# One maximum and one exponential for the longest query tile of an attention, with a new order of its steps

## The chip, the cores and the metric

The kernel runs on one core of a Trainium2 chip. The metric is the time of one execution on the device in microseconds (us). Engines are named as in the profile: PE is TensorE (matrix products, and transposes as products with a unit matrix), DVE is VectorE, ACT is ScalarE, POOL is GpSimd, and SP is SyncE, whose queue issues nearly all of the transfers.

## The reference

Three layers follow one another: a block-causal attention, a dense FFN with an ELU, and a mixture of experts that gives each token to one expert. The change touches the attention alone.

```python
B, H, S, D = 2, 8, 576, 64
scores = np.matmul(q, k.transpose(0, 1, 3, 2)) / np.sqrt(D)
mask = (np.arange(S)[:, None] // 64) >= (np.arange(S)[None, :] // 64)
scores = np.where(mask, scores, -1e9)
scores = scores - np.max(scores, axis=-1, keepdims=True)
attn = np.exp(scores)
attn = attn / (np.sum(attn, axis=-1, keepdims=True) + 1e-09)
x = np.matmul(attn, v)                    # then (1152, 512), all heads side by side
h = x @ w_in                              # (512, 2048)
x = np.where(h > 0, h, np.exp(np.minimum(h, 0)) - 1) @ w_out
...                                       # then the mixture of 8 experts
```

## The kernel before

A matrix product of two float32 operands is made of products of a high and a low part of each (q, k and the values are split so). The 16 heads are worked on in 8 pairs: head a of a pair sits in partitions 0 to 63 of q and k, head b in 64 to 127.

The queries of a head are cut in five tiles of 128 (the first has 64). Tile t has as many keys as the mask leaves it: 64, 192, 320, 448 and 576. The scores lie in PSUM in three parts: part 0 is tile 4, whose 576 keys take two banks of 288 each; part 1 is tile 3 (448 keys) with tile 0 (64 keys) in one bank; part 2 is tiles 2 and 1 (320 and 192 keys) in one bank. With two banks for transposes and two for the values, all eight banks are taken.

The attention's instructions come in an order that is written out by hand: a string of 115 steps, `ORDER`, is worked through once per round, and each engine has its share of the steps in just this order. The last digit of a step says how many pairs it lies behind: round i does step `...1` for pair i-1, so a pair is spread over up to four rounds. There are 11 rounds (0 to 10), of which the middle ones hold all steps. The letter before the last digit is the head. The steps, with the lines of the profile:

- `S` scores (PE, L423; the mask is added by a product of its own, L434); `Spi` is piece i of part p, so `S00` and `S01` are the two banks of tile 4.
- `M` the maximum of a piece over its keys, negated (DVE, `largest`, L445); `M02` is the smaller of the two negated maxima of tile 4 (`largest_of_two`, L452).
- `E` the exponential, with the sum of a row along with it (ACT, `power`, L458).
- `D` the denominators on DVE: `D02` adds the two sums of tile 4 (L465), then `total` adds 1e-9 (L473) and `inverse` inverts (L479).
- `N` the normalization of the probabilities (POOL, L485).
- `T`, `TE` transposes of probabilities on PE (L504, L508, L529), `t`, `te` their evacuation (ACT L495 for t00, t10 and te0, DVE L496 for the others).
- `V` the value products (PE, L545), `X` their evacuation (ACT L560, DVE L87).
- `K` transposes of q and k of the next pair (PE, L370), `k` their split into high and low (ACT L378, DVE L379), `B` the copy of k for both heads (POOL, L339), `L` and `Q` transfers on SP's queue that stack the parts of k and q (L358, L350).
- `c` conversion steps of the FFN's first weights, on ACT, DVE and POOL.

Transfers are issued by the same steps: behind the second `V` of a pair v of a later pair is loaded (L316, L319), behind the second `Q` raw q and k. SP's queue issues one after the other in this order. A step whose input isn't there holds back what stands behind it on its engine. The FFN and the experts come after this, from other code.

Of the kernel before, what the change touches and what calls it, by code (L numbers as in the profile page):

```python
# [9 lines left out]
FP32 = mybir.dt.float32  # L10
# [4 lines left out]
ACTF = mybir.ActivationFunctionType  # L15
# [11 lines left out]
D00a1 S00b1 E20b1 S01b1 M11b1 K0a0 M01b1 N21a1 D01a1 K1a0 M00b1 k00a0 k01a0 X003 k10a0 N11a1 N10a1  # L27
V12 D02a1 E11b1 D20b1 M02b1 E10b1 N00a1 E01b1 k11a0 L0 K0b0 X013 c52 c32 D21b1 k00b0 c73 T1a1 S20a0
S21a0 E00b1 S10a0 S11a0 t11a1 D10b1 k01b0 D11b1 TEa1 M21a0 t10a1 D00b1 M20a0 c62 N20b1 D01b1 c00
M11a0 D02b1 T2a1 te0a1 S00a0 S01a0 t21a1 E20a0 t20a1 T0a1 E21a0 K1b0 M10a0 M00a0 X102 t00a1 k10b0  # L30
M01a0 D20a0 N00b1 N11b1 X112 E10a0 N21b1 V02 k11b0 T0b1 c11 M02a0 N10b1 t00b1 D21a0 S20b0 S21b0 B00
B30 E11a0 T2b1 c41 Q00 c21 E00a0 T1b1 E01a0 B20 t21b1 t20b1 S10b0 S11b0 B10 Q10 t11b1 t10b1 M20b0
M21b0 D10a0 M10b0 TEb1 te0b1 N20a0 E21b0 D11a0
# [9 lines left out]
def attention_ffn_moe(  # L43
# [231 lines left out]
    def part1():  # L275
# [84 lines left out]
        def turn(m, which, g, pool=ps_t, tag="t"):  # L360
# [6 lines left out]
            bank = pool.tile([128, 512], FP32, tag=tag, name="qkT")  # L367
# [39 lines left out]
        def scores(n, part, i):  # L407
# [3 lines left out]
            if c0 == 0:  # L411
                banks[n, part, b] = ps_s.tile([128, 512], FP32, tag=f"s{part}{b}", name="s")
            bank, (q0, nq) = banks[n, part, b], QT[t]
# [27 lines left out]

        def largest(n, part, i):
            t, b, c0, k0, w = PIECES[part][i]
            nq = QT[t][1]
            nc.vector.tensor_reduce(  # L445
                out=stat[n][0][0:nq, t + b:t + b + 1], in_=banks[n, part, b][0:nq, c0:c0 + w], axis=AX.X,
                op=ALU.max, negate=True,
            )

        def largest_of_two(n, t):  # L450
            neg = stat[n][0]
            nc.vector.tensor_tensor(out=neg[:, t:t + 1], in0=neg[:, t:t + 1], in1=neg[:, t + 1:t + 2], op=ALU.min)  # L452

        def power(n, part, i):
            prob[n, part] = PROB[part][n % 2]
            t, b, c0, k0, w = PIECES[part][i]
            nq = QT[t][1]
            nc.scalar.activation(  # L458
                out=prob[n, part][0:nq, c0 + k0:c0 + k0 + w], in_=banks[n, part, b][0:nq, c0:c0 + w], func=ACTF.Exp,
                bias=stat[n][0][0:nq, t:t + 1], accum_out=stat[n][1][0:nq, t + b:t + b + 1],  # L460
            )

        def total_of_two(n, t):
            den = stat[n][1]
            nc.vector.tensor_tensor(out=den[:, t:t + 1], in0=den[:, t:t + 1], in1=den[:, t + 1:t + 2], op=ALU.add)  # L465
# [11 lines left out]
        def inverse(n, part):  # L477
            rd = stat[n][2][:, cols(part)]
            nc.vector.reciprocal(out=rd, in_=rd)  # L479
# [112 lines left out]
        for _ in range(42):  # L592
            nc.tensor.matmul(out=warm[:, 0:128], lhsT=mrow, rhs=mrow, start=True, stop=True)
        for w in "kq":
            for g in range(2):
                for f in turn(0, w, g, ps_s, ("s10", "s20", "s00", "s01")[2 * "kq".index(w) + g]):
                    f()
# [32 lines left out]
        def do(name, h, m):  # L630
# [31 lines left out]
            elif kind == "M":  # L662
                largest_of_two(n, 4) if rest == [0, 2] else largest(n, *rest)
            elif kind == "E":
                power(n, *rest)
            elif kind == "D":
                if rest == [0, 0]:
                    total_of_two(n, 4)
                elif rest[1] == (1 if rest[0] == 0 else 0):
                    total(n, rest[0])  # L670
                else:
                    inverse(n, rest[0])
# [686 lines left out]
```

## Time and profile before

| | before |
| --- | --- |
| median of 3 executions | 496.95 us (495.81 to 499.03) |
| the profiled execution | 498.9 us, of it 496.6 between the first and the last instruction |
| PE busy | 475.1 us (96%) |
| PE's weight loads | 396.1 us (80%) |
| DVE busy | 346.7 us (70%) |
| ACT busy | 308.5 us (62%) |
| POOL busy | 117.2 us (24%) |
| mean granted clock of TensorE, as a share of full speed | 0.994 |

The attention takes the first 110 us or so. Its rounds begin, by the split of a pair's k on ACT, at 8.97, 18.49, 29.76, 41.45, 53.12, 64.79 and 76.45 us. Busy times overlap: an engine takes up an instruction before the last is done, so lengths of neighbours add up to more than the time from start to start. A busy PE waits for nothing, but its ends are modelled. In rows of a timeline the bracket tells how long the engine was idle just before and what it was inferred to wait for.

### The profile page before, as it was taken

Reading aid. Unit: us, or ns where it says so; the run is one execution under the profiler, and the core shown is the slowest. Engines: PE = TensorE matmul, PEld = TensorE weight load, DVE = VectorE, ACT = ScalarE, POOL = GpSimd, SP = SyncE. Lnnn points to the kernel's source line nnn. Section 1 sums busy time; section 2 is a strip of 40 time slices with the busy share of each in tenths; the row PEclk is TensorE's granted clock in tenths of the full one; section 3 lists DMA queues with packets and bytes.
Section 4 is the critical chain, followed back from the end, with each engine's and each line's share of the span. In section 5 each row is a group of like instructions: output and inputs, shape, how many; then the busy total and the mean of one; then the engine's idle time right before and its main releaser. Section 6 shows DMA issues by size and latency. Waiting matters only on the chain. (4 is left out here: it accounts for less than half of the span.)

```text
span 496.6 us, 8643 instructions
## 1 busy us (share of the span) xinstructions
PE 475.1 (96%) x2822; PEld 396.1 (80%) x2822; DVE 346.7 (70%) x841; ACT 308.5 (62%) x696; POOL 117.2 (24%) x209
## 2 busy tenths in 40 slices
PE   6899999999999999999999999999999999999993
PEld 6778887879998898999999888877777777775772
DVE  6789897969978999994373465458378985551560
ACT  4788997867856667654463446437388884642650
POOL 6467877560000000000000020421111331210210
PEclk9999999999999999999999999989999999999999
DMA  8789775503789975341023032529969999350100
GB/s 192 165 206 216 168 173 109 149 21 114 176 241 260 295 264 170 98 128 42 1 85 86 0 107 52 187 79 361 390 208 319 354 364 316 100 215 21 29 26 24
DMA packets 61253, 80.85 MB, mean 163 GB/s; under 512 B 33170, under 2 KB 33170, under 8 KB 61200
## 3 DMA queue, kind: packets, MB, share of 16 engines
q1 hardware_dynamic: 58368, 75.18, 50.7%
q0 software_dynamic: 1632, 4.72, 2.5%
q8 instruction: 28, 0.46, 0.4%
q10 hardware_dynamic: 1200, 0.30, 0.3%
q14 instruction: 25, 0.20, 0.1%
HBM read 62.17 MB, written 12.41 MB: 150 GB/s over the span
## 5 line engine op out<-in xcount | busy, mean ns | idle before, releaser
L260 PE MATMUL acc<-wbh,gh 128*128 128x512 f32 x144 | 57.3, 398 | 0.0
L260 PE MATMUL acc<-wbh,gl 128*128 128x512 f32 x144 | 57.1, 397 | 0.0
L260 PE MATMUL acc<-wbl,gh 128*128 128x512 f32 x144 | 57.1, 397 | 0.0
L916 POOL DMA_INDIRECT disp<-y_all,slot x9 | 9.2, 1019 | 200.6 <-DVE e L245 177.9
L485 POOL TENSOR_SCALAR prob<-prob,stat 128x576 f32<-128x576 f32 (+3 forms) x80 | 42.3, 542 | 27.8 <-DVE stat L479 18.6
L458 ACT ACTIVATE prob<-s,stat 128x288 f32<-128x288 f32 (+4 forms) x96 | 45.3, 480 | 1.5 <-POOL kk L339 0.8
L243 ACT ACTIVATE e<-h 128x384 f32<-128x384 f32 x48 | 23.3, 485 | 36.5 <-PE h L233 34.1
L87 DVE TENSOR_TENSOR xl<-ra,xh 128x1024 fp32r<-128x1024 f32 (+1 forms) x36 | 39.3, 1100 | 8.8 <-ACT xh L1128 6.9
L186 DVE SCALAR_TENSOR_TENSOR cv_t<-r,cv_t 128x512 int32<-128x512 int32 x64 | 44.1, 690 | 0.3
L1262 POOL DMA_INDIRECT out<-o,gt x12 | 17.0, 1413 | 112.2 <-DVE o L1261 68.8
L233 PE MATMUL h<-xh,wah 128*128 128x384 f32 x192 | 42.2, 341 | 0.8 <-DVE e L245 0.8
L233 PE MATMUL h<-xl,wah 128*128 128x384 f32 x192 | 41.6, 337 | 0.0
L245 DVE SCALAR_TENSOR_TENSOR e<-e,h 128x384 f32<-128x384 f32 x48 | 26.4, 549 | 21.3 <-ACT e L244 21.1
L233 PE MATMUL h<-xh,wal 128*128 128x384 f32 x192 | 41.1, 336 | 0.0
L445 DVE TENSOR_REDUCE stat<-s 128x1 f32<-128x288 f32 (+4 forms) x96 | 37.6, 422 | 2.8 <-PE s L434 1.6
L1229 PE MATMUL acc<-xh,gh 128*128 128x512 f32 (+1 forms) x96 | 39.4, 411 | 0.0
L1128 ACT ACTIVATE xh<-ra 128x1024 fp32r<-128x1024 f32 (+1 forms) x36 | 34.4, 963 | 7.3 <-PE h L233 2.8
L87 DVE TENSOR_TENSOR xl<-rb,xh 128x1024 fp32r<-128x1024 f32 (+1 forms) x36 | 38.8, 1099 | 0.1
L233 PEld LDWEIGHTS h<-xh,wah 128*128 128x128 f32 x192 | 34.2, 188 | 5.7 <-DVE e L245 1.7
L1229 PE MATMUL acc<-xh,gl 128*128 128x512 f32 (+1 forms) x96 | 37.9, 395 | 0.0
L1229 PE MATMUL acc<-xl,gh 128*128 128x512 f32 (+1 forms) x96 | 37.9, 395 | 0.0
L87 DVE TENSOR_TENSOR gl<-hT,gh 128x512 fp32r<-128x512 f32 (+1 forms) x24 | 15.8, 657 | 29.9 <-ACT gh L1223 29.8
(173 smaller groups left out, 1165.9 us busy)
## 6 DMA issues: line engine op xcount, KB each, us to landing
ra<-in_moe_w SPq DMA_DIRECT2D x32, 512.0 KB, 5.3
rb<-in_moe_w SPq DMA_DIRECT2D x32, 512.0 KB, 6.6
r<-in_moe_w_in SPq DMA_DIRECT2D x16, 512.0 KB, 5.1
r<-in_moe_w_out SPq DMA_DIRECT2D x16, 512.0 KB, 4.4
disp<-z SPq DMA_DIRECT2D x18, 257.0 KB, 7.2
rows<-disp SPq DMA_DIRECT2D x14, 257.0 KB, 3.6
out<-z SPq DMA_DIRECT2D x9, 256.0 KB, 4.9
kr<-in_k SPq DMA_DIRECT2D x16, 128.0 KB, 2.8
```

Of the source, the lines that this page charges most:

```text
L87: eng.tensor_tensor(out=lo, in0=x, in1=hi.bitcast(FP32), op=ALU.subtract)
L186: nc.vector.scalar_tensor_tensor(out=st["t"], in0=x(), scalar=scalar, in1=st["t"], op0=op, op1=ALU.bitwise_or)
L233: nc.tensor.matmul(out=h[:, f, :], lhsT=w[:, kk, (f0 + f) * 128:(f0 + f + 1) * 128], rhs=x[:, kk, t0:t0 + n], start=(i == 0), stop=(i == l ...
L243: nc.scalar.activation(out=e, in_=hf, func=ACTF.Relu, scale=-1.0)
L245: nc.vector.scalar_tensor_tensor(out=e, in0=e, scalar=-1.0, in1=hf, op0=ALU.add, op1=ALU.max)
L260: nc.tensor.matmul(out=acc[t], lhsT=x[:, f, t * 128:(t + 1) * 128], rhs=w[:, f0 + f, :], start=(first and f == 0 and i == 0), stop=(last a ...
L445: nc.vector.tensor_reduce(out=stat[n][0][0:nq, t + b:t + b + 1], in_=banks[n, part, b][0:nq, c0:c0 + w], axis=AX.X, op=ALU.max, negate=True,)
L458: nc.scalar.activation(out=prob[n, part][0:nq, c0 + k0:c0 + k0 + w], in_=banks[n, part, b][0:nq, c0:c0 + w], func=ACTF.Exp, bias=stat[n][0 ...
L485: nc.gpsimd.tensor_scalar(out=p, in0=p, scalar1=stat[n][2][0:nq, t:t + 1], scalar2=0.0, op0=ALU.mult, op1=ALU.add)
L1128: lambda: nc.scalar.activation(out=hi, in_=r, func=ACTF.Copy),
L1229: nc.tensor.matmul(out=acc[0:n], lhsT=x[:, f % 4, 0:n], rhs=y[:, f % 2, :], start=(f == 0 and i == 0), stop=(f == NF - 1 and i == 2),)
L1262: nc.gpsimd.indirect_dma_start(out=views[e * CT + j], out_offset=bass.IndirectOffsetOnAxis(ap=gate[e][0:n, j, 1:2].bitcast(I32), axis=0), ...
```

## The change

Tile 4's two banks become one PSUM tile `[128, 2, 512]`. One reduction over both axes gives the maximum of 576 scores, and one activation all 576 exponentials and their sum; `largest_of_two` and `total_of_two` go, and with them the steps M01, M02, E01 and D02. The prologue takes its four banks from a list that is put up first; they are the same banks in the same order. The 107 steps that are left stand in a new order. In it all steps keep the digit that says in which round they are done, that is, a step moves within its round alone.

```diff
--- before.py
+++ after.py
@@ -24,13 +24,12 @@
 
 
 ORDER = """
-D00a1 S00b1 E20b1 S01b1 M11b1 K0a0 M01b1 N21a1 D01a1 K1a0 M00b1 k00a0 k01a0 X003 k10a0 N11a1 N10a1
...
+D00a1 N21a1 S00b1 K0a0 k00a0 S01b1 k01a0 c73 N11a1 N10a1 D01a1 K1a0 c52 V12 E20b1 k10a0 E10b1 B00
...
 """
 
 ON_ACT = {"t00", "t10", "te0"}
@@ -357,14 +356,15 @@
                 own = slice(64 * h, 64 * h + 64)
                 nc.sync.dma_start(out=KLO[m % 2][own, h].bitcast(FP32), in_=kT[m][1][own].bitcast(FP32))
 
-        def turn(m, which, g, pool=ps_t, tag="t"):
+        def turn(m, which, g, bank=None):
 
             src, dst, sc = (qraw, qT, SCALE) if which == "q" else (kraw, kT, 1.0)
             if g == 0:
                 dst[m] = tuple(qt_p.tile([128, S], F32R, tag=which + x, name=which + x) for x in "hl")
             js = range(NK)[2 * g:2 + (NK - 2) * g]
             a, e = 128 * js[0], min(S, 128 * (js[-1] + 1))
-            bank = pool.tile([128, 512], FP32, tag=tag, name="qkT")
+            if bank is None:
+                bank = ps_t.tile([128, 512], FP32, tag="t", name="qkT")
             ps = bank[:, 0:e - a]
             for j in reversed(js):
                 nc.tensor.transpose(
@@ -408,9 +408,9 @@
 
             m, h = divmod(n, 2)
             t, b, c0, k0, w = PIECES[part][i]
-            if c0 == 0:
-                banks[n, part, b] = ps_s.tile([128, 512], FP32, tag=f"s{part}{b}", name="s")
-            bank, (q0, nq) = banks[n, part, b], QT[t]
+            if c0 == 0 and b == 0:
+                banks[n, part] = ps_s.tile([128, 2 if part == 0 else 1, 512], FP32, tag=f"s{part}", name="s")
+            bank, (q0, nq) = banks[n, part][:, b], QT[t]
 
             wq = 128
             if m:
@@ -439,30 +439,25 @@
 
             return mask
 
+        def whole(n, part, i):
+
+            t, c0 = parts[part][i]
+            nb, w = split(t)
+            return banks[n, part][0:QT[t][1], 0:nb, c0:c0 + w], slice(t, t + 1), slice(0, QT[t][1])
+
         def largest(n, part, i):
-            t, b, c0, k0, w = PIECES[part][i]
-            nq = QT[t][1]
-            nc.vector.tensor_reduce(
-                out=stat[n][0][0:nq, t + b:t + b + 1], in_=banks[n, part, b][0:nq, c0:c0 + w], axis=AX.X,
-                op=ALU.max, negate=True,
-            )
-
-        def largest_of_two(n, t):
-            neg = stat[n][0]
-            nc.vector.tensor_tensor(out=neg[:, t:t + 1], in0=neg[:, t:t + 1], in1=neg[:, t + 1:t + 2], op=ALU.min)
+            s, t, r = whole(n, part, i)
+            nc.vector.tensor_reduce(out=stat[n][0][r, t], in_=s, axis=AX.XY, op=ALU.max, negate=True)
 
         def power(n, part, i):
             prob[n, part] = PROB[part][n % 2]
-            t, b, c0, k0, w = PIECES[part][i]
-            nq = QT[t][1]
+            s, t, r = whole(n, part, i)
+            c0 = parts[part][i][1]
+            nk = s.shape[1] * s.shape[2]
             nc.scalar.activation(
-                out=prob[n, part][0:nq, c0 + k0:c0 + k0 + w], in_=banks[n, part, b][0:nq, c0:c0 + w], func=ACTF.Exp,
-                bias=stat[n][0][0:nq, t:t + 1], accum_out=stat[n][1][0:nq, t + b:t + b + 1],
+                out=prob[n, part][r, c0:c0 + nk].rearrange("q (b w) -> q b w", b=s.shape[1]), in_=s, func=ACTF.Exp,
+                bias=stat[n][0][r, t], accum_out=stat[n][1][r, t],
             )
-
-        def total_of_two(n, t):
-            den = stat[n][1]
-            nc.vector.tensor_tensor(out=den[:, t:t + 1], in0=den[:, t:t + 1], in1=den[:, t + 1:t + 2], op=ALU.add)
 
         def cols(part):
             ts = [t for t, _ in parts[part]]
@@ -591,9 +586,11 @@
         warm = ps_v.tile([128, half], FP32, tag="v0", name="warm")
         for _ in range(42):
             nc.tensor.matmul(out=warm[:, 0:128], lhsT=mrow, rhs=mrow, start=True, stop=True)
+        free = [ps_s.tile([128, x, 512], FP32, tag=f"s{i}", name="qkT") for i, x in ((1, 1), (2, 1), (0, 2))]
+        free = [x[:, i] for x in free for i in range(x.shape[1])]
         for w in "kq":
             for g in range(2):
-                for f in turn(0, w, g, ps_s, ("s10", "s20", "s00", "s01")[2 * "kq".index(w) + g]):
+                for f in turn(0, w, g, free.pop(0)):
                     f()
         load_qk(2)
         for _ in range(4):
@@ -660,16 +657,11 @@
                 if name != "S20":
                     pend[n, name]()
             elif kind == "M":
-                largest_of_two(n, 4) if rest == [0, 2] else largest(n, *rest)
+                largest(n, *rest)
             elif kind == "E":
                 power(n, *rest)
             elif kind == "D":
-                if rest == [0, 0]:
-                    total_of_two(n, 4)
-                elif rest[1] == (1 if rest[0] == 0 else 0):
-                    total(n, rest[0])
-                else:
-                    inverse(n, rest[0])
+                (inverse if rest[1] else total)(n, rest[0])
             elif kind == "N":
                 norm(n, *rest)
             elif kind == "T":
```

What the string of steps moves is seen on the engines. First SP's queue in round 5 (`kl` and `qq` are the stacked low k and the stacked q of the next pair, the first two `qq` being head a's, `v_114` the values of a later pair, `r` raw FFN weights). Before:

```order
L151 DMA r<-in_moe_w_in 128x2x512
L358 DMA kl_125<-kl 64x576 x2
L316 DMA v_114<-in_v 128x4x64 x2
L319 DMA v_114<-in_v 64x2x64
L350 DMA qq<-qh 64x576
L350 DMA qq<-ql 64x576
L350 DMA qq<-qh 64x576
L350 DMA qq<-ql 64x576
```

and in the changed kernel:

```order
L150 DMA r<-in_moe_w_in 128x2x512
L357 DMA kl_125<-kl 64x576 x2
L349 DMA qq<-qh 64x576
L349 DMA qq<-ql 64x576
L315 DMA v_114<-in_v 128x4x64 x2
L318 DMA v_114<-in_v 64x2x64
L349 DMA qq<-qh 64x576
L349 DMA qq<-ql 64x576
```

Head a's two transfers of q moved ahead of the three that load v.

Second, DVE in round 1 (`stat` are columns of maxima, sums and inverses; `kl` is the low part of k, first 256 columns and then 320). Before:

```order
L473 TENSOR_SCALAR stat_165<-stat_164 128x1
L445 TENSOR_REDUCE stat_166<-s 128x1
L379 SCALAR_TENSOR_TENSOR kl<-qkT,kh 128x256
L479 RECIPROCAL stat_165<-stat_165 128x1
L473 TENSOR_SCALAR stat_168<-stat_167 128x2
L452 TENSOR_TENSOR stat_166<-stat_166 128x1
L379 SCALAR_TENSOR_TENSOR kl<-qkT,kh 128x320
```

and in the changed kernel:

```order
L468 TENSOR_SCALAR stat_165<-stat_164 128x1
L379 SCALAR_TENSOR_TENSOR kl<-qkT,kh 128x256
L474 RECIPROCAL stat_165<-stat_165 128x1
L379 SCALAR_TENSOR_TENSOR kl<-qkT,kh 128x320
L450 TENSOR_REDUCE stat_166<-s 64x1
L450 TENSOR_REDUCE stat_166<-s 128x1
```

The first `kl` has moved ahead of a maximum of 288 keys, the second stands with one inverse ahead of it, and the maxima come behind both.

Third, PE in a round with all its steps (`pT` and `pE` are transposed probabilities, `s` scores with their number of keys, `xT` values, `mcol,mrow` the mask). Before, head b's part, from behind the values on:

```order
L508 MATMUL pT<-ident,prob_118 128x128 x4
L423 MATMUL s<-kk,qq 128x320
L423 MATMUL s<-kl_125,qq 128x320
L423 MATMUL s<-kk,qq 128x192
L423 MATMUL s<-kl_125,qq 128x192
L434 MATMUL s<-mcol,mrow 128x64
L434 MATMUL s<-mcol,mrow 128x64
L508 MATMUL pT<-ident,prob_122 128x128 x3
L504 MATMUL pT<-ident,prob_120 128x128
L508 MATMUL pT<-ident,prob_120 128x128 x3
L423 MATMUL s<-kk,qq 128x448
L423 MATMUL s<-kl_125,qq 128x448
```

and in the changed kernel:

```order
L423 MATMUL s<-kk,qq 128x320
L423 MATMUL s<-kl_125,qq 128x320
L503 MATMUL pT<-ident,prob_118 128x128 x4
L423 MATMUL s<-kk,qq 128x192
L423 MATMUL s<-kl_125,qq 128x192
L434 MATMUL s<-mcol,mrow 128x64
L434 MATMUL s<-mcol,mrow 128x64
L503 MATMUL pT<-ident,prob_122 128x128 x3
L423 MATMUL s<-kk,qq 128x448
L423 MATMUL s<-kl_125,qq 128x448
L434 MATMUL s<-mcol,mrow 128x64
```

The transposes of `prob_118` (T0b) now stand between the 320-key and the 192-key scores of the next head instead of ahead of both, and the 448-key scores follow the transposes of `prob_122` where they followed those of `prob_120`.

On POOL two of the four `kk` (B) moved ahead of the normalization N00a, which they followed, and all four ahead of N00b.

## Rows read from the trace of the kernel before

**Rows 1.** Table by stretches: length; busy PE, PEld, DVE, ACT, POOL; clock; DMA share; GB/s.

```profile
53.12:64.79 11.67, 11.67 (x106) 9.42 (x107) 10.20 (x42) 10.58 (x40) 9.71 (x16) 1.00 0.66 152
...
76.45:88.10 11.65, 10.42 (x93) 8.19 (x93) 8.78 (x34) 9.37 (x34) 8.26 (x12) 1.00 0.41 92
```

**Rows 2.** PE's timeline in a steady round: start, length, engine, line, operation, names, shape.

```profile
55.31 0.27 PE L504 MATMUL pT<-ident,prob 128*128 128x128 f32 x1
55.42 0.49 PE L508 MATMUL pT<-ident,prob 128*128 128x128 f32 x3
...
56.31 0.45 PE L423 MATMUL s<-kk,qq 128*128 128x448 f32 x1
56.59 0.36 PE L423 MATMUL s<-kl,qq 128*128 128x448 f32 x1
56.80 0.20 PE L434 MATMUL s<-mcol,mrow 128*128 128x64 bf16 x1
...
57.06 0.66 PE L529 MATMUL pE<-ident,prob 128*128 128x128 f32 x4
...
58.45 0.63 PE L508 MATMUL pT<-ident,prob 128*128 128x128 f32 x4
...
60.36 0.65 PE L508 MATMUL pT<-ident,prob 128*128 128x128 f32 x4
60.77 0.39 PE L423 MATMUL s<-kk,qq 128*128 128x320 f32 x1
...
63.33 0.38 PE L423 MATMUL s<-kk,qq 128*128 128x288 f32 x1
```

**Rows 3.** PE's timeline, rounds 0 and 1; in brackets idle before and releaser.

```profile
19.40 0.44 PE L370 MATMUL qkT<-ident,qr 128*128 128x128 f32 x2 [0.58 <-DVE kl L379]
20.09 0.30 PE L504 MATMUL pT<-ident,prob 128*128 128x128 f32 x1 [0.25 <-DVE stat L479]
...
24.65 0.63 PE L508 MATMUL pT<-ident,prob 128*128 128x128 f32 x4 [0.44 <-POOL prob L485]
...
27.92 0.63 PE L529 MATMUL pE<-ident,prob 128*128 128x128 f32 x4 [0.51 <-DVE pt L496]
```

**Rows 4.** PE's timeline, the start of round 6.

```profile
80.47 0.38 PE L423 MATMUL s<-kk,qq 128*128 128x320 f32 x1 [1.23 <-DMA qq<-ql]
```

**Rows 5.** SP's queue in time, rounds 5 and 6: start and length of the issue.

```profile
72.12 1.08 SPq L316 DMA_DIRECT2D v<-in_v  x2
73.26 0.65 SPq L319 DMA_DIRECT2D v<-in_v  x1
...
74.65 0.56 SPq L350 DMA_DIRECT2D qq<-ql  x1
```

**Rows 6.** DMA view of the stretch 69 to 82 us.

```profile
DMA packets 3389, 2.33 MB, mean 179 GB/s; under 512 B 2620, under 2 KB 2620, under 8 KB 3388
```

**Rows 7.** Groups by line and shape, ACT, 30 to 100 us: busy us, mean ns.

```profile
L458 ACT ACTIVATE prob<-s,stat 128x288 f32<-128x288 f32 x24 | 11.8, 495 | 0.0
L458 ACT ACTIVATE prob<-s,stat 128x448 f32<-128x448 f32 x12 | 7.8, 649 | 0.0
```

**Rows 8.** The same view, DVE.

```profile
L445 DVE TENSOR_REDUCE stat<-s 128x1 f32<-128x288 f32 x25 | 10.6, 448 | 0.0
L445 DVE TENSOR_REDUCE stat<-s 128x1 f32<-128x448 f32 x12 | 7.3, 611 | 0.0
...
L452 DVE TENSOR_TENSOR stat<-stat 128x1 f32<-128x1 f32 x12 | 2.7, 228 | 0.0
```

**Rows 9.** ACT's timeline, the steady round from 53.12.

```profile
61.11 0.59 ACT L495 COPY pt<-pT 128x512 f32<-128x512 f32 x1 [0.34 <-PE pT L508]
```

**Rows 10.** DVE's timeline, the start of round 1.

```profile
18.57 0.45 DVE L445 TENSOR_REDUCE stat<-s 128x1 f32<-128x288 f32 x1
18.93 0.41 DVE L379 SCALAR_TENSOR_TENSOR kl<-qkT,kh 128x256 fp32r<-128x256 f32 x1
...
19.46 0.48 DVE L379 SCALAR_TENSOR_TENSOR kl<-qkT,kh 128x320 fp32r<-128x320 f32 x1
```

**Rows 11.** POOL's timeline, rounds 1 and 2.

```profile
24.62 3.15 POOL L339 TENSOR_SCALAR kk<-kh 64x576 fp32r<-64x576 f32 x4
```

**Rows 12.** Table by stretches, the FFN's first 28 us (columns as in rows 1).

```profile
112.00:140.00 28.00, 28.00 (x145) 25.54 (x144) 26.87 (x63) 21.50 (x43) 0.29 (x1) 1.00 0.61 151
```

More of the change, by code (lines that the diff above doesn't have):

```diff
@@ L26 @@
 ORDER = """
-D00a1 S00b1 E20b1 S01b1 M11b1 K0a0 M01b1 N21a1 D01a1 K1a0 M00b1 k00a0 k01a0 X003 k10a0 N11a1 N10a1
[L28 to L33, printed above, removed]
+D00a1 N21a1 S00b1 K0a0 k00a0 S01b1 k01a0 c73 N11a1 N10a1 D01a1 K1a0 c52 V12 E20b1 k10a0 E10b1 B00
+k11a0 K0b0 T1a1 X003 S20a0 M11b1 L0 M00b1 E11b1 D20b1 k00b0 B20 N00a1 X013 D10b1 k01b0 D21b1 S10a0
+B30 S21a0 D11b1 t11a1 c32 TEa1 E00b1 t10a1 c00 N11b1 D00b1 T2a1 S00a0 c62 S11a0 D01b1 N10b1 M21a0
+M20a0 te0a1 E21a0 t21a1 t20a1 M11a0 M10a0 T0a1 E20a0 S01a0 c11 t00a1 K1b0 N21b1 D20a0 k10b0 E11a0
+B10 D21a0 k11b0 M00a0 N00b1 Q00 N20b1 V02 S20b0 T0b1 E10a0 X102 X112 t00b1 S21b0 T2b1 M21b0 t20b1
+S10b0 t21b1 E00a0 T1b1 c41 D10a0 S11b0 t10b1 Q10 t11b1 M20b0 M10b0 c21 N20a0 D11a0 TEb1 te0b1 E21b0
 """
```

## The prediction

> **What bounds the kernel now.** I read the page first, for the shares: TensorE (PE) is busy in nearly the whole span. A share is an average, so next came the table by stretches, cut at the starts of the attention's rounds. A steady round takes 11.67 us, and in the round from 53.12 PE is busy for all 11.67 of it, while VectorE (DVE) has 10.20, ScalarE (ACT) 10.58 and GpSimd (POOL) 9.71 [rows 1]. So there is nothing to wait for there: the round lasts as long as PE's list of instructions. The round from 76.45 is the exception, with 10.42 busy in 11.65 [rows 1]. Third, PE's timeline shows where PE does wait in the attention: four times in rounds 0 and 1, for 0.58 + 0.25 + 0.44 + 0.51 = 1.78 us [rows 3], and once in round 6, for 1.23 us on a transfer of low q parts [rows 4]. Between these places the change can only alter what PE's own list costs. After the attention, the FFN's first stretch has PE busy for 28.00 of 28.00 us and DVE for 26.87 [rows 12].
>
> The profiled execution took 498.9 us (span 496.6 and 2.3 around it); the median of the three runs is 496.95. I make the sum as a difference on the profiled execution and set it off from the median.
>
> **The merged maximum and exponential.** For the longest tile (576 keys in two banks) a head now has one maximum and one exponential of 576 columns in place of two of 288, and the minimum and the addition that joined the halves are gone. An exponential of 288 columns takes 495 ns, one of 448 takes 649 [rows 7]: 0.96 ns a column, so 576 columns make about 0.77 us by the slope, against 2 x 0.495 = 0.99. Bounds, since no such instruction stands in the trace: 0.65 (as the one of 448) and 0.99 (nothing saved); I take 0.77, and the slope is the nearest row's. For the maximum it is 448 and 611 ns [rows 8], 1.02 ns a column, hence 0.74 against 0.90; bounds 0.61 and 0.90. So 0.2 us of ACT and, with the minimum's 0.228 [rows 8], some 0.4 of DVE come free per head. The price of this on the path is nothing in a steady round, because PE's own 11.67 us cover it [rows 1]; without that cover it would be up to 0.6 us a head.
>
> What the merge costs is that both banks come free only at the end of the long exponential. In the steady round t00b (ACT, 0.59 us) starts at 61.11 [rows 9]. In the new order T0b stands behind S20b, whose two matmuls take about 0.39 [rows 2], so t00b starts near 61.5; E00a follows directly, near 62.0, and ends near 62.75. The next S00b, the first to need these banks, starts at 63.33 [rows 2]. That leaves 0.6 us, so I take 0; if the cover were gone it would cost PE what is missing, each round.
>
> **The new order on PE.** PE has the same instructions, but in other neighbourhoods, and where PE is the bound each costs. Four transposes that stand among transposes last about 0.49 + 0.11 = 0.60 (three last 0.49, and the step from the one ahead is 0.11). Four that follow the 64-column score last 0.66, four behind a mask 0.63, four behind the value matmuls 0.65 [rows 2]. A 448-column score that follows a mask holds PE for 0.28 to the next start, the one behind it 0.21 [rows 2], so 0.07 more. Before, a round has two runs behind a 64-column score (TEa, TEb: 0.12), three behind a mask (K0a, T0a, T2b: 0.09), two behind values (K0b, T0b: 0.10) and S10a behind a mask (0.07): 0.38. After: two behind a 64-column score (T0a, TEb: 0.12), five behind a mask (K1a, TEa, K1b, T2b, T1b: 0.15), one behind values (K0b: 0.05), and four for which no row stands: K0a behind a 288-column score and T0b behind a 320-column one (0 to 0.06 each), S21a behind a mask (0 to 0.07), S20b behind values (0 to 0.11, the upper end being 0.05 and 0.06 together). That is 0.32 + (0 to 0.30). The difference is -0.06 to +0.24 per round. I take 0.12, above the middle, because every change of kind that has a row costs something. Over seven bound rounds: **+0.85 us** (-0.4 to +1.7).
>
> The Trainium skill, "TensorE: Matmul & The Clock Gate", section "Back-to-back issue gap", has the steady spacing set by the weight load and the streaming of each matmul together, and none of it by what kind of matmul stood before. By it the new list costs what the old did, and the sum would be 0.85 lower. The rows differ by 0.03 to 0.06 for runs of the same four transposes [rows 2], so I keep my term, and the free list is a rival.
>
> **Rounds 0 and 1.** These wait on DVE. Before, the second kl part (L379) stands behind the maximum, an inverse, a total and the minimum, and the first, at 18.93, behind a maximum [rows 10]; PE waits for it at 19.40 (0.58), and at 20.09 (0.25, put down to the statistics, but the bank of K1a is read by the second kl until about then) [rows 3]. In the new order the first kl follows D00a at once and the second has one inverse ahead of it. Both waits should go: -0.83. The other two don't. POOL's doublings of k (B, four in 3.15 us, so 0.79 each [rows 11]) now stand between its normalizations: two ahead of N00a, all four ahead of N00b. TEa, T0a and T0b wait for those, and I expect the 0.44 and 0.51 to stay and about 0.3 to come on top, since each N is preceded by 1.6 to 3.1 us of doublings that used to follow them, but starts earlier by the maximum saved. Sum **-0.5 us** (bounds -1.78, all gone, and +0.8, one doubling exposed).
>
> **Round 6.** On SP's queue the first stack of q (Q00) now stands ahead of the load of v. In round 5 v is issued at 72.12 and the low q part of the first head at 74.65 [rows 5]. v is 288 KB (two transfers of 128 and one of 32), and at this stretch's mean of 179 GB/s [rows 6] that is 1.6 us. Taken out of the way, the data that ended PE's wait at 80.47 land near 78.9; PE would have gone on at 80.47 - 1.23 = 79.24 [rows 4]. So the wait goes: **-1.2 us** (bounds 0 and -1.23). v is needed a round later, and the second head's q, still behind v, only for S20b, some 5 us on. If that cover fails the stall returns there.
>
> Everything after the attention keeps its instructions; its few swaps of neighbours I cost at nothing, since PE is full there [rows 12]. If DVE's 1.1 us of slack in that stretch didn't cover them, up to 0.9 would come back, as below.
>
> **Sum.** -0.5 - 1.2 + 0.85 = -0.85: 498.9 becomes 498.05 for this execution, and 496.95 becomes **496.1**.
>
> **The rivals.**
> *The transfer still comes late.* The 512 KB of FFN weights and kl stay ahead of Q00 on the queue, and the margin worked out above is only 0.3 us. Then -1.2 falls away: 497.3.
>
> *Slower: a new wait in each steady round.* Place: PE at TEa, for POOL's N00a behind two doublings, or at S00b, for the merged banks. POOL is busy 9.71 us of 11.67 [rows 1], and each doubling is 0.79 in a row that T, V and S hang on. A miss of 0.3 to 0.6 us in seven rounds costs 2.1 to 4.2: 498.2 to 500.3, middle 499.2; it decides from 0.12 a round (0.85 / 7). Against it: 0.6 us of room at S00b, and the maximum and exponential end sooner. Beside it stands the Trainium skill, "Perfetto Trace Analysis", section "Matmuls" under "Optimizing Tensor Performance": independent groups of matmuls should rotate through banks, so that one's evacuation overlaps the next one's matmuls. Tying two banks together goes against that; by the rule S01b no longer starts under the second exponential.
>
> *PE's list costs no more than before:* -1.7, 495.25. For it: the lower bound above is negative.
>
> *All of rounds 0 and 1 goes:* -1.78 instead of -0.5, 494.8. The doublings in POOL's row speak against it.
>
> *Given back.* The FFN starts earlier, but DVE converts its weights at 26.87 us of 28 [rows 12] and the weights come when they come: 496.95, no change.
>
> **How the numbers follow.** Forecast 0.36, late transfer 0.14, new waits 0.22, free list 0.12, early rounds 0.05, given back 0.11. The range leaves out the upper half of the new waits (0.11) and about 0.05 below: with the early rounds and the free list together 494.0, and with the middle of the new waits 499.2. A measurement of this kernel tells about 1% (5 us) from no change. Slower by that takes 0.8 us of new wait in each of seven rounds, above the rival's span: 0.06. Faster by that takes more than all the waits of the attention together (1.78 + 1.23 = 3.0): 0.03. The rest, 0.91, is the same.
>
> **What would show it.** The stretch of a steady round should read 11.75 to 11.85 with PE full; PE without waits there means the merge is covered. The wait of round 6 should be gone, with Q00 ahead of v on the queue. Of the early waits those on kl should go and those on POOL stay. An exponential of 576 columns should read 0.7 to 0.85. I am wrong if steady rounds show idle time of PE before TEa, T0b or S00b, or if PE is full and the round is 0.3 longer.

## The result, and the profile after

The changed kernel took a median of 502.21 us (501.32 to 502.29, four runs) against 496.85 for the kernel before on the same chip: 1.008 times as long, with a 95% interval of 1.0056 to 1.0104. That is 5.4 us more, where 0.85 less was forecast, and 3 us above the end of the range (499.2). Run a second time, beside its repairs, it took 1.0074 times the time before (1.0046 to 1.0102).

The page of the changed kernel, its span and the shares of the engines:

```profile
span 500.6 us, 8591 instructions
PE 477.7 (95%) x2822; PEld 396.1 (79%) x2822; DVE 347.3 (69%) x793; ACT 308.3 (62%) x664; POOL 114.3 (23%) x209
```

The work is the same on PE (2822 matmuls) and less on DVE and ACT in instructions (793 instead of 841, 664 instead of 696). Yet PE's busy time grew by 2.6 us, and DVE's by 0.6. The table by stretches for three steady rounds, in the columns of [rows 1]:

```profile
43.07:55.37 12.30, 12.13 (x107) 9.42 (x105) 10.75 (x38) 10.54 (x36) 9.54 (x15) 1.00 0.77 195
55.37:67.61 12.24, 12.15 (x107) 9.45 (x104) 10.74 (x37) 10.53 (x35) 7.81 (x14) 1.00 0.60 138
67.61:79.91 12.30, 12.13 (x107) 9.43 (x105) 10.72 (x38) 10.54 (x36) 9.53 (x15) 1.00 0.81 189
```

A round takes 12.24 to 12.30 us instead of 11.67 [rows 1], and PE is still shown as nearly full (12.13 of 12.30). The first row to hold against that is PE's timeline in the middle of such a round. First the kernel before, where two masks and the transposes TEa stand at other places of the list, then the changed one:

```profile
56.24 0.23 PE L434 MATMUL s<-mcol,mrow 128*128 128x64 bf16 x2
56.31 0.45 PE L423 MATMUL s<-kk,qq 128*128 128x448 f32 x1
...
57.06 0.66 PE L529 MATMUL pE<-ident,prob 128*128 128x128 f32 x4
57.55 0.49 PE L508 MATMUL pT<-ident,prob 128*128 128x128 f32 x3
```

```profile
59.31 0.23 PE L434 MATMUL s<-mcol,mrow 128*128 128x64 bf16 x2
59.59 0.63 PE L524 MATMUL pE<-ident,prob 128*128 128x128 f32 x4
60.26 0.55 PE L503 MATMUL pT<-ident,prob 128*128 128x128 f32 x3
60.56 0.38 PE L423 MATMUL s<-kk,qq 128*128 128x288 f32 x1
```

Two masks hold PE for 0.07 us where nothing waits (56.24 to 56.31 in the kernel before); here 0.28 us pass until TEa's transposes start. Four transposes hold it for 0.49 (57.06 to 57.55 before); here 0.67 pass until T2a's. No bracket stands on either row. A transpose has a length of 0.27 us in the profile and lets the next one start after 0.11 [rows 2], so a wait of up to 0.16 us behind one is counted as busy time; the same holds behind the two masks, which show 0.23 us and let the next start after 0.07. Lengths told me in the prediction that PE was full; only starts tell whether it waits.

So I measured every step by the time from its first matmul to the first of the next step. From this come the starts of S00b in each round, from PE's timeline of each kernel (us; "before, again" is the kernel before, profiled a second time):

| kernel | first score | S00b, r2 | r3 | r4 | r5 | r6 | r7 | r8 | last value matmul |
| --- | --- | --- | --- | --- | --- | --- | --- | --- | --- |
| before | 10.68 | 28.30 | 39.99 | 51.66 | 63.33 | 74.99 | 88.15 | 98.69 | 110.53 |
| before, again | 10.78 | 28.41 | 40.10 | 51.77 | 63.44 | 75.10 | 86.77 | 97.31 | 109.16 |
| changed | 12.40 | 30.03 | 41.77 | 54.07 | 66.31 | 78.61 | 90.91 | 101.62 | 114.03 |
| own bank in the prologue | 10.71 | 28.36 | 40.11 | 52.41 | 64.66 | 77.03 | 89.29 | 100.00 | 112.42 |
| additions of one column | 12.35 | 30.07 | 41.81 | 53.79 | 65.63 | 77.61 | 89.45 | 100.05 | 112.65 |
| both | 10.73 | 28.46 | 40.20 | 52.18 | 64.03 | 76.12 | 87.99 | 98.60 | 111.20 |
| all repairs | 11.04 | 28.70 | 40.45 | 52.42 | 64.17 | 76.19 | 87.94 | 98.72 | 110.79 |
| new order, split | 10.22 | 27.97 | 40.10 | 52.44 | 64.70 | 77.02 | 89.29 | 102.06 | 114.64 |
| old order, merged | 10.12 | 27.47 | 39.20 | 50.85 | 62.50 | 74.15 | 85.79 | 96.32 | 108.08 |

Against the kernel before as profiled again, the changed one is 1.62 late at the first score, still 1.62 at round 2, then loses 0.05, 0.63, 0.57, 0.64 and 0.63 in rounds 2 to 6, 0.17 in round 7 and 0.80 in round 8, wins 0.24 in the last steps, and is 4.87 late at the last value matmul. What comes behind the attention keeps most of this: the spans differ by 4.3 us (500.6 to 496.3). From the last value matmul to the end, executions of one and the same kernel differ by 1 to 2 us (386.1 and 387.1 for the kernel before, 386.6 and 384.6 for the changed one), so the table is where the causes are to be read.

New waits carry it, at three places. **In the prologue**, PE's timeline (in brackets the idle time before and the inferred releaser):

```profile
6.97 0.38 PE L370 MATMUL qkT<-ident,qr 128*128 128x128 f32 x2
9.20 0.55 PE L370 MATMUL qkT<-ident,qr 128*128 128x128 f32 x3 [1.85 <-DVE qz L379]
...
12.40 0.39 PE L423 MATMUL s<-kh,qz 128*128 128x320 f32 x1
```

The last three transposes of pair 0's q wait until DVE has taken the first two out. The two groups lie in different banks, as before, but the banks are now the two halves of one tile, and in the changed program these transposes have a wait for DVE. Behind it the wait for k's low part, which stands in both kernels, is shorter (1.68 us instead of 2.25).

**In rounds 3 to 6**, DVE's and POOL's timelines at the place of TEa (the same round as above):

```profile
58.03 0.26 DVE L468 TENSOR_SCALAR stat<-stat 128x2 f32<-128x2 f32 x1
58.19 0.45 DVE L86 TENSOR_TENSOR xl<-xT,xh 128x288 fp32r<-128x288 f32 x1
58.56 0.57 DVE L468 TENSOR_SCALAR stat<-stat 128x2 f32<-128x2 f32 x1
59.03 0.41 DVE L379 SCALAR_TENSOR_TENSOR ql<-qkT,qh 128x256 fp32r<-128x256 f32 x1
59.37 0.21 DVE L474 RECIPROCAL stat<-stat 128x2 f32<-128x2 f32 x2
59.50 0.19 DVE L491 COPY pt<-pT 64x64 f32<-64x64 f32 x1
59.62 0.13 DVE L468 TENSOR_SCALAR stat<-stat 128x1 f32<-128x1 f32 x1
```

```profile
56.84 1.42 POOL L338 TENSOR_SCALAR kk<-kh 64x576 fp32r<-64x576 f32 x2
58.36 0.75 POOL L480 TENSOR_SCALAR prob<-prob,stat 128x576 f32<-128x576 f32 x1
59.19 0.67 POOL L338 TENSOR_SCALAR kk<-kh 64x576 fp32r<-64x576 f32 x1
```

L468 adds 1e-9 to two denominators, 128x2 numbers. At 58.56 it takes 0.57 us and ends at 59.13; POOL's N00a ends at 59.11. The one at 58.03 ends at 58.29, and POOL's doubling at 58.26. The addition of a single column at 59.62 takes 0.13 while POOL works beside it. Behind the stalled addition stand k01 of q (59.03 to 59.44), whose bank TEa needs, and t11 (59.50 to 59.69), for which ACT's t10 waits in both kernels (its row here: 59.73, idle for 0.57 before, released by DVE's L491); t10 ends at 60.21, and T2a, which needs that bank, starts at 60.26. Held against a round of the same order without waits (all repairs, round 4), PE falls behind at these two places alone: TEa starts 0.20 to 0.29 us later in rounds 3 to 6, T2a's transposes another 0.2 to 0.3, and the round is 0.49 to 0.55 us longer.

**In round 1**, PE waits for DVE and then for POOL:

```profile
21.64 0.30 PE L499 MATMUL pT<-ident,prob 128*128 128x128 f32 x1 [0.63 <-DVE kl L379]
...
25.91 0.31 PE L423 MATMUL s<-kl,qq 128*128 128x320 f32 x1
27.43 0.66 PE L503 MATMUL pT<-ident,prob 128*128 128x128 f32 x4 [1.21 <-POOL prob L480]
```

The second is T0b, in place of the last two waits of [rows 3] (0.44 at T0b and 0.51 at TEb). Of the two on kl (0.58 and 0.25) the first is gone; the second, at T1a, has grown to 0.63. DVE's row of this second kl names ACT's split of k as what it waits for:

```profile
21.01 0.49 DVE L379 SCALAR_TENSOR_TENSOR kl<-qkT,kh 128x320 fp32r<-128x320 f32 x1 [0.42 <-ACT kh L378]
```

Together they come to 1.84 us, where the four came to 1.78.

The merged instructions cost what the slopes of [rows 7, 8] gave (0.77 and 0.74):

```profile
L457 ACT ACTIVATE prob<-s,stat 128x576 f32<-128x576 f32 x12 | 8.9, 743 | 0.3 <-DVE stat L450 0.3
...
L450 DVE TENSOR_REDUCE stat<-s 128x1 f32<-128x576 f32 x12 | 8.9, 742 | 0.0
```

### The profile page after: what moved, and what is told of

Read it like the earlier page. It is cut to its first block, busy times and chain, and to the rows that moved or that the text cites. A ratio compares the mean times of both kernels' runs of the same rounds, so it can differ in the third digit from the quotient of the medians.

```text
span 500.6 us, 8591 instructions
## 1 busy us (share of the span) xinstructions
PE 477.7 (95%) x2822; PEld 396.1 (79%) x2822; DVE 347.3 (69%) x793; ACT 308.3 (62%) x664; POOL 114.3 (23%) x209
## 5 line engine op out<-in xcount | busy, mean ns | idle before, releaser
L457 ACT ACTIVATE prob<-s,stat 64x64 f32<-64x64 f32 (+3 forms) x80 | 41.7, 524 | 5.1 <-DVE stat L450 3.2
L450 DVE TENSOR_REDUCE stat<-s 64x1 f32<-64x64 f32 (+3 forms) x80 | 35.7, 477 | 3.9 <-PE s L434 1.3
```

The lines of the kernel that those rows point to most:

```text
L450: nc.vector.tensor_reduce(out=stat[n][0][r, t], in_=s, axis=AX.XY, op=ALU.max, negate=True)
L457: nc.scalar.activation(out=prob[n, part][r, c0:c0 + nk].rearrange("q (b w) -> q b w", b=s.shape[1]), in_=s, func=ACTF.Exp, bias=stat[n][0] ...
```

## The experiments

In what follows "x1.0xx" is the ratio to the kernel before on the same chip.

### The kernel before, once more

No edit.

> The kernel before, profiled once more. Theory C (the wait of 1.47 us for q in round 6 belongs to the one execution that was profiled, not to the kernel): T1a to S20a of round 6 takes 0.36 us as in the other rounds, and all other steps of the attention stay within 0.05. Rival (it is in every execution): 1.5 to 1.9 us again.

PE's timeline from T1a to S20a in round 6, and the table by stretches for that round:

```profile
78.86 0.49 PE L508 MATMUL pT<-ident,prob 128*128 128x128 f32 x3
79.11 0.39 PE L423 MATMUL s<-kk,qq 128*128 128x320 f32 x1
```

```profile
76.56:88.20 11.64, 11.64 (x109) 9.32 (x110) 10.17 (x42) 10.56 (x39) 9.69 (x16) 1.00 0.50 117
```

The wait of [rows 4] isn't there: the step takes 0.36 us, 1.47 less, and every other step of rounds 0 to 9 is within 0.04 of the first profile. SP issues in the same order, the low q part of head a 0.8 us later than in [rows 5]. The merge alone, below, issues in the old order and hasn't got the wait either. So it belonged to one execution, and theory C holds; why the transfer came late in that one, and how often it does, is not shown.

### Head a's q ahead of v, alone

```diff
-... N21b1 V02 k11b0 T0b1 ... c41 Q00 c21 ...
+... N21b1 k11b0 Q00 V02 T0b1 ... c41 c21 ...
```

> The kernel before, with one step moved: the stack of head a's q (Q00) and the split it needs (k11b0) stand ahead of V02, so that SP issues head a's two q transfers ahead of the load of v, as in the changed kernel. Theory (the wait of round 6 is only the place in the queue): the 1.47 us between the transposes of T1a and the scores S20a of round 6 go, all else stays, 495.4. Rival (v, or head b's q, now comes late instead): a wait of 0.5 us or more appears at V1 or S20b in rounds 6 or 7, and the time stays within 0.7 of 496.85.

x0.9992 (0.9976 to 1.0007). No wait in round 6, none elsewhere. Since the kernel before has none there either in its second profile, this edit had nothing to take away; the expectation of 1.47 us less fails, as the prediction's 1.2 does.

### The prologue's fourth bank from another pool

```diff
-        free = [x[:, i] for x in free for i in range(x.shape[1])]
+        free = [x[:, 0] for x in free] + [ps_v.tile([128, 512], FP32, tag="v1", name="qkT")]
```

> The changed kernel, with the prologue's fourth bank (second part of q of pair 0) taken from the value banks, so that it shares no PSUM tile with the first part of q; nothing else differs. Theory A (the two transposes of q wait for each other's evacuation because both banks are one tile): the wait of 1.85 us at 9.20 goes, the first score starts at about 10.7 instead of 12.4, and the whole kernel takes 1.7 us less, 500.5. Rival (what the prologue loses is made up by a later wait that exists anyway, in round 0 or 1): the first score starts earlier, but round 2 starts at about 30.0 as in the changed kernel, and the time stays at 502.2.

x1.0053 (1.0034 to 1.0072). PE's timeline in the prologue:

```profile
6.78 0.71 PE L370 MATMUL qkT<-ident,qr 128*128 128x128 f32 x5
...
10.71 0.39 PE L423 MATMUL s<-kh,qz 128*128 128x320 f32 x1
```

All five transposes of q run in one go, the first score starts 1.69 earlier, and the lead is still 1.61 at the last value matmul. Nothing behind makes it up. Theory A holds.

### Additions of one column

```diff
-            nc.vector.tensor_scalar(
-                out=stat[n][2][:, d], in0=stat[n][1][:, d], scalar1=1e-9, scalar2=None, op0=ALU.add
-            )
+            for t in range(d.start, d.stop, d.step or 1):
+                nc.vector.tensor_scalar(
+                    out=stat[n][2][:, t:t + 1], in0=stat[n][1][:, t:t + 1], scalar1=1e-9, scalar2=None, op0=ALU.add
+                )
```

> The changed kernel, with the addition of 1e-9 to two denominators at once (DVE, 128x2) written as two additions of 128x1; nothing else differs. Theory B (the 128x2 addition stands still until the POOL instruction beside it ends, 569 ns where a free one takes 150; behind it k01 and t11 come late, and PE's TEa and T2a wait for them): additions of about 0.13 us each, the waits ahead of TEa and T2a fall from about 0.45 us a round to under 0.1, rounds 3 to 6 take 11.8 to 11.9 us instead of 12.27, and the kernel takes 1.5 to 1.9 us less, 500.5. Rival (the round's 12.27 us are PE's own list in its new neighbourhoods): rounds stay within 0.1 of 12.27 and the time at 502.2.

x1.0069 (1.0041 to 1.0096). DVE, POOL and PE at the place of TEa:

```profile
57.75 0.20 DVE L469 TENSOR_SCALAR stat<-stat 128x1 f32<-128x1 f32 x2
...
58.24 0.20 DVE L469 TENSOR_SCALAR stat<-stat 128x1 f32<-128x1 f32 x2
58.36 0.41 DVE L379 SCALAR_TENSOR_TENSOR ql<-qkT,qh 128x256 fp32r<-128x256 f32 x1
```

```profile
58.08 0.75 POOL L481 TENSOR_SCALAR prob<-prob,stat 128x576 f32<-128x576 f32 x1
```

```profile
59.04 0.23 PE L434 MATMUL s<-mcol,mrow 128*128 128x64 bf16 x2
59.11 0.63 PE L525 MATMUL pE<-ident,prob 128*128 128x128 f32 x4
59.59 0.55 PE L504 MATMUL pT<-ident,prob 128*128 128x128 f32 x3
```

Two additions now take 0.20 us together while N00a runs beside them, where one took 0.57. k01 follows at 58.36, 0.12 behind the additions' start instead of 0.47, and TEa starts 0.07 behind the masks: its wait is gone. Rounds 3 to 6 take 11.98, 11.84, 11.98 and 11.84 us, against 12.24 to 12.30: 1.5 us less in four rounds. The wait at T2a shrank but stayed in every other round (0.15). At the last value matmul 1.38 us are won; 1.5 to 1.9 were expected. The time itself doesn't show it (the ratio's interval overlaps that of the changed kernel); the mechanism is what the trace shows.

### Both repairs

Both edits above.

> The changed kernel with both repairs: the prologue's fourth bank from the value banks, and the additions of 1e-9 as 128x1. Theory (the two causes are independent and add): first score at 10.7, rounds 3 to 6 of 11.85 to 12.0, together 3.0 to 3.5 us less than the changed kernel, 0.1 to 0.4 % above the kernel before. Rival (the later waits move in when the earlier go): less than 2.2 us.

x1.0018 (0.9997 to 1.0039). The two add, nearly: at the last value matmul 1.61 and 1.38 us alone, 2.83 together. What is left against the kernel before is 2.0 us there.

### The maximum M11b where it stood

```diff
-... c52 V12 E20b1 k10a0 E10b1 ... S20a0 M11b1 L0 M00b1 ...
+... c52 V12 E20b1 k10a0 M11b1 E10b1 ... S20a0 L0 M00b1 ...
```

> The changed kernel with one step moved: the maximum M11b (64 keys) stands ahead of the exponential E10b, as in the kernel before, so that it no longer waits on DVE for E10b through the shared tile of statistics. Theory E (that wait holds up DVE's list, and the stalled addition lands beside N00a because of it): in a steady round M11b starts at 0.1 to 0.6 us earlier, the addition ahead of k01 falls between two POOL instructions or is stalled by less, the waits ahead of TEa and T2a shrink by 0.2 to 0.4 us a round, and the end of the attention (TEa of round 8, 0.5 us) recovers: 1.3 to 2.2 us less than the changed kernel. Rival (only the addition matters): rounds 3 to 6 stay at 12.2 to 12.3 us, at most 0.6 us less.

x1.007 (1.0044 to 1.0096). DVE and POOL in a steady round:

```profile
57.75 0.61 DVE L468 TENSOR_SCALAR stat<-stat 128x2 f32<-128x2 f32 x1
...
58.63 0.57 DVE L468 TENSOR_SCALAR stat<-stat 128x2 f32<-128x2 f32 x1
59.10 0.41 DVE L379 SCALAR_TENSOR_TENSOR ql<-qkT,qh 128x256 fp32r<-128x256 f32 x1
```

```profile
56.91 1.42 POOL L338 TENSOR_SCALAR kk<-kh 64x576 fp32r<-64x576 f32 x2
58.43 0.75 POOL L480 TENSOR_SCALAR prob<-prob,stat 128x576 f32<-128x576 f32 x1
```

Theory E falls. M11b no longer waits for ACT and DVE comes to the first addition 0.35 us earlier by POOL's clock (57.75, 0.84 behind the start of the doublings, where it was 1.19). There it stands until 58.36, when the doubling ends (58.33), and the second addition until 59.20, when N00a ends (59.18). k01 starts where it did. This is the strongest evidence for theory B: DVE arrives earlier and gains nothing; both additions end 0.02 to 0.03 us behind POOL's instruction.

### Two doublings of k behind the normalizations

```diff
-... S10a0 B30 S21a0 ... N11b1 D00b1 ... N10b1 M21a0 ... E11a0 B10 D21a0 ... N00b1 Q00 ...
+... S10a0 S21a0 ... N11b1 D00b1 ... N10b1 B30 M21a0 ... E11a0 D21a0 ... N00b1 B10 Q00 ...
```

> The changed kernel with two of the four doublings of k moved on POOL: B30 behind N10b and B10 behind N00b (they stood ahead of N00a and N00b). Theory D (T0b's wait of round 1 is for N00b, which POOL reaches late because of the doublings): S20b to T0b in round 1 takes 0.4 to 0.7 us instead of 1.75, round 2 starts about 1.1 us earlier, 1 us less in all. Rival (another input of that stretch is as late): T0b or the next scores wait as long, and round 2 starts within 0.3 us of 30.0.

x1.0077 (1.0047 to 1.0106). In the profiled execution TensorE's granted clock was 0.50 (the lower of its two levels, 1.2 GHz) from 10 to 15 us, so only steps behind round 0 are read. PE's timeline in round 1:

```profile
28.10 0.66 PE L503 MATMUL pT<-ident,prob 128*128 128x128 f32 x4 [0.39 <-POOL prob L480]
...
29.49 0.55 PE L503 MATMUL pT<-ident,prob 128*128 128x128 f32 x3 [0.45 <-POOL prob L480]
```

T0b's wait shrinks from 1.21 to 0.39 us, and one of 0.45 appears at T2b, for the next normalization behind the moved doubling. From S00b of round 1 to that of round 2 it is 11.26 us instead of 11.43. Theory D names the place rightly and not the price: POOL is late as a whole in round 1, and moving its work moves the wait. The rival is the better reading.

### The order alone, with two maxima and two exponentials

The kernel before with the new string, in which M00, E00 and the additions are written out again:

```diff
-... M00b1 E11b1 ... E00b1 t10a1 ... D00b1 T2a1 ... D01b1 ...
+... M00b1 M01b1 M02b1 E11b1 ... E00b1 E01b1 t10a1 ... D00b1 D01b1 T2a1 ... D02b1 ...
```

> The new order alone: the kernel before (two maxima, two exponentials, the joining minimum and addition, two tiles of one bank) with its steps in the new order, the second maximum, the minimum, the second exponential and the addition right behind the first. Theory (the order costs, the merge doesn't): no prologue wait, but rounds of 12.27 us or more (DVE has 0.4 us and ACT 0.2 us more per head ahead of k01 and t11), 2 to 6 us above the kernel before. Rival (the merge costs): rounds of at most 11.85, within 1 us of the kernel before.

x1.0103 (1.0068 to 1.0138). No prologue wait (first score at 10.22), rounds 3 to 6 of 12.34, 12.26, 12.32 and 12.27 us, and a further 2.2 us lost in round 7 and 1.0 in round 8. The order costs, with or without the merge; with the halves split it costs more at the end.

### The merge alone, in the old order

The changed kernel with the string of before, and the prologue's fourth bank from the value banks; the string is shown against that of the kernel before:

```diff
-... M11b1 K0a0 M01b1 N21a1 D01a1 K1a0 M00b1 ... V12 D02a1 E11b1 D20b1 M02b1 E10b1 N00a1 E01b1 ...
+... M11b1 K0a0 N21a1 D00a1 K1a0 M00b1 ... V12 D01a1 E11b1 D20b1 E10b1 N00a1 ...
```

> The merge alone: the old order of steps without M01, M02, E01 and D02, with the merged maximum and exponential, and the prologue's fourth bank from the value banks. Theory (the merge is hidden in the steady rounds): rounds of 11.67 us as before and 496.9 within 0.6 (rounds 0 and 1 may gain up to 0.6). Rival (two banks that come free together make PE wait): S00b or S01b start 0.3 us or more late in each of seven rounds, 499 or more.

x0.9977 (0.9959 to 0.9995). The table by stretches for a steady round:

```profile
52.31:63.96 11.65, 11.65 (x106) 9.44 (x107) 10.03 (x36) 10.21 (x36) 9.59 (x16) 1.00 0.71 164
```

PE is as full as in [rows 1], ACT and DVE have less to do, and no step waits for the merged banks. Rounds 0 and 1 gain 0.28 us. The merge alone makes the kernel 0.2% faster, just clear of no change. Additions of 128x2 are held up here too, and more often: 15 of the 32 take over 0.2 us (up to 0.61), against 12 in the changed kernel and 8 in the one before. So a stall needn't cost anything; what stands behind it decides.

### All repairs, and the best order

The changed kernel with both repairs, M11b as above, and t11 right behind k01 of q:

```diff
-... S20a0 M11b1 L0 ... X013 D10b1 k01b0 D21b1 S10a0 B30 S21a0 D11b1 t11a1 c32 ...
+... S20a0 L0 ... X013 D10b1 k01b0 t11a1 D21b1 S10a0 B30 S21a0 D11b1 c32 ...
```

> The changed kernel with all repairs: the prologue's fourth bank from the value banks, additions of 1e-9 as 128x1, M11b ahead of E10b, and t11 right behind k01 of q. Theory: rounds 3 to 6 of 11.75 to 11.8 us, what PE's list in the new order costs without waits; the attention ends within 0.5 us of the kernel before without its wait in round 6, and the time is within 0.8 us of the kernel before. Rival: a further wait shows, rounds above 11.9.

x1.0010 (0.9987 to 1.0032). Rounds 4 and 6 take 11.75 us and have no wait left; rounds 3 and 5 take 11.97 and 12.02, with 0.2 to 0.3 us at S20a and S10a that I did not follow further.

The merge in the old order as above, with two more edits (additions of one column, and q ahead of v):

```diff
-... N21b1 V02 k11b0 T0b1 ... c41 Q00 c21 ...
+... N21b1 k11b0 Q00 V02 T0b1 ... c41 c21 ...
```

> The merge in the old order, with the prologue's fourth bank from the value banks, the additions as 128x1 and head a's q ahead of the load of v on SP's queue. Theory: like the merge alone, since nothing of this is on the path of a usual execution: rounds of 11.67 us, 0.3 us less in rounds 1 and 2, 0 to 0.4 % below the kernel before. Rival: moving q delays v or head b's q, 0.5 us or more lost in a round.

x0.9965 (0.9940 to 0.9990). Round 1 is 0.75 us shorter than in the kernel before and round 2 0.21 longer; rounds 3 to 7 are within 0.04. What round 1 has lost is the wait at TEb, 0.51 in [rows 3]. It is 0.51 with q ahead of v alone and 0.38 with the merge alone, so most of it goes, as far as these runs part the edits, with the additions of one column: in the kernel before, one of 128x2 stands from 24.68 for 0.63 us beside a doubling, ahead of the evacuation that TEb waits for. The ratio is the lowest of all, 0.35% below the kernel before; its interval overlaps that of the merge alone.

### The changed kernel, once more

No edit.

> The changed kernel once more, on the same chip as its repairs. Theory: the same to the nanosecond up to the end of the attention (rounds 3 to 6 of 12.24 to 12.30 us, first score at 12.4), 1.0 % above the kernel before. Rival: as with the wait of round 6 of the kernel before, some of its waits belong to one execution and are gone.

x1.0074. First score at 12.25, rounds 3 to 6 of 12.33, 12.26, 12.32 and 12.27 us, the last value matmul at 113.96. Its waits, unlike that of [rows 4], stand in both profiles.

## Why the prediction was wrong

**The step that failed** is the sentence that, between the waits listed, the change "can only alter what PE's own list costs": it put new waits at nothing, in steady rounds and in the prologue. Measured are 0.49 to 0.55 us of new wait in each of rounds 3 to 6, 2.1 us in all, and 1.6 us in the prologue. Of the -1.7 us that were to come off, 1.2 weren't there to be taken and 0.5 didn't come.

**What bounds the kernel: right for the kernel before, too coarse for the change.** A steady round is PE's list, 11.67 us in both profiles. But I took "PE busy" for "PE doesn't wait", which a wait of less than 0.16 us behind a transpose or a mask escapes. The sign I had set for being wrong did come: PE shown as nearly full, and the round over 0.3 us longer.

**The merge: right.** 0.743 and 0.742 us against 0.77 and 0.74 worked out, hidden in a steady round; the merge alone is 0.2% faster, where I gave it 0.

**"The same banks in the same order" cost 1.6 us.** I costed the prologue at nothing without naming what hides it, because the banks were the same. They were, but two of them were now one tile, and the wait came in front of everything, where nothing behind made it up (1.69 us at the first score, 1.61 at the end, by the repair). What failed is the step from "same bank" to "same waits": the changed program has PE wait for DVE at these transposes.

**The new order on PE: right in sign, small.** The term was 0.12 us a round. Round 2 of the changed kernel has no new wait and takes 11.74 us against 11.69, so the list costs 0.05; the rounds of all repairs without waits take 11.75 against 11.67. Over seven rounds that is 0.4 to 0.6 us, not 0.85. Single steps move by 0.08 to 0.09 us either way (between the first two products of a 192-column score 0.17 us instead of 0.09, of a 448-column score 0.21 instead of 0.29), but their sum nearly cancels. The Trainium skill's rule in "TensorE: Matmul & The Clock Gate" ("Back-to-back issue gap"), which sets the spacing by weight load and streaming and has no term for neighbours, is off by these 0.05 to 0.08 us a round, my term by 0.04 to 0.07: the rounds don't decide between them.

**Rounds 0 and 1: POOL's part right, kl's wrong.** I let the 0.44 and 0.51 stay and 0.3 come on top, 1.25 us behind POOL, and T0b waits 1.21. But of the 0.83 on kl only 0.2 went: I looked at what stands ahead of the second kl on DVE and not at ACT's split, for which it now waits, so that T1a waits 0.63. From the first score to round 2 both kernels take 17.6 us; the sum is 0 instead of -0.5, inside the bounds I gave. The list of waits was also short by one of 0.30 in round 0, at 15.72, which the changed kernel hasn't got.

**Round 6: the wait was real and not the kernel's.** I took 1.2 us off the median for a wait that one profile shows. The kernel before hasn't got it in its second profile, and the edit by itself gains nothing; no run but that one shows the term. A wait on a transfer that one round has and its five neighbours haven't should have gone into the chances, not into the sum. It also hid a part of the loss: the two first profiles differ by 4.0 us, the medians by 5.4.

**The new waits: the rival, with another cause.** The rival on the other side had a wait at TEa of 0.3 to 0.6 us a round and 22% of the chance; measured are 0.49 to 0.55 us in four rounds at TEa and T2a. I put it down to N00a behind the doublings on POOL. The rows show POOL only as the one that holds DVE: an addition of 128x2 that starts while a POOL instruction runs ends 0.02 to 0.03 us behind it in 13 of 16 cases of the changed kernel, and what DVE has behind it is late. The merge was to set some 0.4 us of DVE free per head; DVE's busy time in a steady round rose instead, from 10.20 to 10.7 us. In the kernel before, 8 of the 32 additions of 128x2 last 0.22 to 0.63 us, where free ones take 0.15, and of PE's waits in [rows 3] the one at TEb stands behind such an addition. Making the addition free took the wait at TEa away; bringing DVE there earlier didn't. That the order and not the merge brings this about, the two runs that part them show: 12.3 us a round against 11.65.

The Trainium skill states this: "SBUF — State Buffer", section "Who interferes with whom", has VectorE and GpSimd share a pair of ports that one instruction holds to its end, and names `tensor_scalar`, the addition's form, among those of VectorE that can take it. "VectorE: DVE Perf Modes", section "Mode 2×_2P — use both read ports for one tensor", gives the conditions: one tensor, in SBUF, split in half along an even dimension. The traces agree: 128x2 stalls (0.57 to 0.61 us), 128x1 does not (0.13). The reciprocals of 128x2 next to it, which the first page's list doesn't name, don't stall (0.07 from start to start). Neither page was weighed in the prediction against the order in which POOL's work was moved.

**The end of the attention.** Rounds 7 and 8 lose 1.0 us, 0.7 with all repairs; the prediction put them at nothing, and which step is the cause stays open. M11b's wait on ACT is seen there (DVE idle for 0.60 us at 104.17) but taking it away gained nothing.

## What to carry to other kernels

When an order of steps is changed, read what each engine runs beside the moved work as well as what it waits for: an instruction that is off the path can hold another engine's until it ends. Two buffers made into one can be one buffer for every wait, also in places that use only half, as the prologue did here. And measure a full engine by the starts of its instructions, and a wait on a transfer by more than one execution, before either goes into a sum.

## What the runs showed of the hardware that was not expected

An addition of 128x2 on VectorE in SBUF mostly waits out the GpSimd instruction that runs beside it and ends 0.02 to 0.03 us later (59.13 behind 59.11, 58.29 behind 58.26, 58.36 behind 58.33, 59.20 behind 59.18). Of the 16 in the changed kernel that start beside one, 13 do so; two, at 50.17 and 74.71, end 0.54 us ahead of it after 0.15, and why is not shown. The same addition in two instructions of 128x1 takes 0.20 us in all beside the same work, and none of the 43 of 128x1 that start beside a GpSimd instruction in that run takes over 0.16. A transfer wait of 1.2 us can stand in one execution of a program and be missing in the next, while all steps around it agree to 0.04 us.
